# Attention and a two-layer MLP on one core: the SBUF pools allocated in another order

## The chip, the cores and the metric

One NeuronCore of one Trainium2 chip runs the kernel. The metric is the device time of one execution in microseconds (us); lower is better. Times of several runs are given by their median.

## What is computed

The reference takes `q`, `k`, `v` of shape (4, 8, 768, 64), two whole numbers `n_global` = 8 and `n_local` = 96, and two weight matrices. It computes masked attention, then an MLP over the 3072 x 512 result. Cut to what matters:

```
scores = q @ k.T / sqrt(64) + bias(head, distance)     # 1e9 below where not local or global
x      = softmax(scores) @ v                           # as 3072 x 512
h      = x @ w_in                                      # 512 x 2048, the first layer
g      = h * sigmoid(h)
out    = g @ w_out                                     # 2048 x 512, the second layer
```

The program calls this MLP the MoE part, hence the names.

## The kernel before, in words

**Tiles.** The 3072 tokens are 24 blocks `i` of 128, and two blocks make one of 12 groups `g` of 256 tokens. The weights are taken from HBM as 64-bit numbers and turned into a high part and a low part, each a float32r tile kept in SBUF for the whole run: `WIH` and `WIL` (lines 211, 212) for the first layer, `WOH`, `WOL` and two short tiles `w_last` for the second (line 219, `w_o`). The activations are split likewise, so every product is a sum of three matmuls: high with high, low with high, high with low.

**A matmul.** `nc.tensor.matmul(out, a, b)` first loads `a`, here always 128 columns, into the array as the stationary operand (the trace calls it LDWEIGHTS, on the row PEld) and then streams `b`, the moving operand, past it (MATMUL, on the row PE). The trace writes `out<-moving,stationary`.

**First layer.** `pair_h` (line 931, the matmuls are on line 938) has the weights `WIH` and `WIL` stationary and the 256 tokens of the group moving, from the tiles `xh` and `xl` made by `x_part` (line 696). For a pair of feature blocks there are 24 matmuls of 256 columns. The first two groups go through `moe_h` (line 831, matmuls on line 836), with the same operands.

**Gate.** `pair_tanh`, `pair_gate` and `pair_sum` (lines 942 to 956) make the gated activations in a tile `sg` on ScalarE (ACT), VectorE (DVE) and GpSimd (POOL); `pair_high` (line 965) and `pair_low` (line 971) split them into `gh` and `gl`.

**Second layer.** `pair_o` (line 986, matmuls on line 996) has `gh` or `gl` stationary and the weights moving: `WOH`, `WOL`, `w_last`, and sums of weights that are loaded from DRAM for each pair into `tx` and `ty`. Each is 256 columns wide, apart from 72 of 512 columns. The first two groups go through `moe_o` (line 856, matmuls on line 861, 512 columns) with `ghs` and `gls` stationary.

**Attention.** `stack_scores` (line 573, matmuls on line 580) streams `KH` and `KL`, 232 columns (128 in the first block of a batch), past `QH`, `QL` and `R`; each pair of heads lies 928 bytes after the one before in `KH` and `KL`. `turn` and `turn_p` transpose with the tile `ident` moving; `values` multiplies with `v`.

**Order.** A planner (`Plan`, line 50) with a cost and a rank for each step fixes, while the program is built, the order in which every engine gets its instructions. Nothing in it depends on where a tile lies. All large DMAs are issued on the SP queue.

**Places.** Each `tile_pool` takes a stretch of SBUF in every partition, and the stretches lie one behind the other in the order in which the pools are made (lines 196 to 204: `flag`, `const`, `sb2`, `sb3`). In a pool, the tiles of each tag lie behind those of the tag that was asked for first, and a size is rounded up to 32 bytes. A place below is a number of bytes in a partition, modulo 512.

Of the kernel before, what the change touches and what calls it, by code (L numbers as in the profile page):

```python
# [10 lines left out]
F32 = mybir.dt.float32  # L11
F32R = mybir.dt.float32r
BF16 = mybir.dt.bfloat16
I16 = mybir.dt.int16
I32 = mybir.dt.int32
# [6 lines left out]
P = 128  # L22
NPREV = 96
NG = 8
WIN = NPREV + NG + P
# [155 lines left out]
def attn_moe(ctx, tc, q, k, v, n_global, n_local, w_in, w_out, out):  # L181
    nc = tc.nc
    B, H, S, D = q.shape
    NT, DM = out.shape
    DFF = w_in.shape[1]
    NHP = H // 2
    NJ = S // P
    NCC = DM // P
    NFC = DFF // P
    NB = 2  # L190
    GT = NB * P
# [8 lines left out]
    ctx.enter_context(fast)  # L200
    ctx, outer = fast, ctx
    const = ctx.enter_context(tc.tile_pool(name="const", bufs=1))
    sb2 = ctx.enter_context(tc.tile_pool(name="sb2", bufs=2))
    sb3 = ctx.enter_context(tc.tile_pool(name="sb3", bufs=3))
    psum = ctx.enter_context(tc.tile_pool(name="psum", bufs=1, space=PSUM))
    dram = ctx.enter_context(tc.tile_pool(name="dram", bufs=1, space=bass.MemoryType.DRAM))

# [11 lines left out]
    def w_o(i, f):  # L219
# [5 lines left out]
                const.tile([P, NLAST, DM], F32R, name=f"w_last{x}", tag=f"last{x}") for x in range(2)  # L225
            )
        return last_w[i][:, f - (NFC - NLAST)]
    NM = const.tile([P, B * NJ * H], F32, name="NM")
    banks = [psum.tile([P, 512], F32, name=f"bank{i}") for i in range(8)]

    def bank(b, n=None, c=None):
# [3 lines left out]
        return x[:, :n] if c is None else x[:, :n * c].rearrange("p (n c) -> p n c", n=n)  # L235


    B1 = const.tile([P, NHP, WIN], BF16, name="B1")
    B0 = const.tile([P, NHP, P], BF16, name="B0")

    st = {}
    raw = const.tile([P, 2, 2], I32, name="raw")
    nc.gpsimd.memset(raw, 0)

    def scalars():
# [6 lines left out]

    def places():

        t1 = sb2.tile([P, 1024], F32, name="t1", tag="xh")
        t2 = sb2.tile([P, 1024], F32, name="t2", tag="xl")
        bias_t.extend(t1[:, i * WIN:(i + 1) * WIN] for i in range(3))
        bias_t.extend(t2[:, i * P:(i + 1) * P] for i in range(3))
        st["ones"] = [t2[:, i * P:(i + 1) * P] for i in (3, 4)]
        R, col = bias_t[0], bias_t[3]  # L260
        io = dict(allow_small_or_imprecise_dtypes=True)
        nc.gpsimd.iota(R[:, cur], [[-1, P]], base=0, channel_multiplier=1, **io)
        nc.gpsimd.iota(col, [[1, P]], base=0, channel_multiplier=0, **io)
        nc.gpsimd.iota(R[:, prev], [[-1, NPREV]], base=NPREV, channel_multiplier=1, **io)
        for x, c in zip(st["ones"], (1.0, 4294967296.0)):
            nc.gpsimd.memset(x, c)
# [47 lines left out]


    assert H == 8
    few = const.tile([P, 32], F32, name="few")
    assert B * NJ - PAR["VC"] // 2 <= 20
    VT, twice = few[:, :B * NJ - PAR["VC"] // 2], few[:, 20:21]
    nc.vector.memset(twice[:D], 1.0)  # L320
# [2 lines left out]
    def bias_of(first, hp):  # L323
        eng = nc.gpsimd if hp >= PAR["BP"][first] else nc.vector
        o, x = ((B0, bias_t[5]) if first else (B1, bias_t[2]))
        eng.tensor_scalar(o[:, hp], x, -(2.0 ** (-8.0 * (2 * hp + 1) / H)) / SC, None, ALU.mult)

    TOP = const.tile([P, 2, 2 * NFC], I16, name="TOP")  # L330
    first_gh = sb2.tile([P, NB, GT], F32R, name="ghs", tag="GH", bufs=1)
    first_gl = sb2.tile([P, NB, GT], F32R, name="gls", tag="GL", bufs=1)
    first_th = [sb2.tile([P, 2, 2 * GT], F32, name=f"ths{x}", tag="SG") for x in range(2)]
    lent_pt = [first_th[0][:, 1], first_th[1][:, 0], first_th[1][:, 1]]
    warm = first_th[0][:, 0, :P].bitcast(BF16)
    nc.vector.memset(warm, 0.0)
# [3 lines left out]
        SG=2, GH=1, GL=1, str=2, ty=2, ob=2, tt=3, ck=1,  # L340
# [47 lines left out]
    def lent(n):  # L388
        return n % 5 - 3 if n < PAR["NX"] and n % 5 > 2 else None
# [42 lines left out]
    for n in range(2 * NFC):  # L432
        rank = PAR["C0"] + PAR["CR"] * n
        a, m, x = [] if lent(n) is not None else [Buf("big")], Buf("mid", "m"), lent(n)
# [15 lines left out]
    def check(n, i):  # L450
        top = st["c", n].bitcast(I16).rearrange("p f w -> p (f w)").rearrange("p (f w) -> p f w", w=4)[:, :, 3]
        nc.vector.tensor_reduce(
            TOP[:, i, n:n + 1], top, AX.X, (ALU.min, ALU.max)[i], apply_absolute_value=True
        )
# [31 lines left out]
    xt = {}  # L486
# [112 lines left out]
    def cols(i):  # L599
        return (0 if i % NJ else C1), (WIN if i % NJ else P)  # L600
# [13 lines left out]
    def top_of(i, hp, a):  # L614
        t = blk[i]
        if not a:
            x = sb3.tile([P, 512], F32, name="pe", tag="m", bufs=NM2)
            t["p", hp] = x[:, :2 * WIN].rearrange("p (a n) -> p a n", a=2)
            x = sb3.tile([P, 4], F32, name="sm", bufs=4)
            t["sum", hp], t["inv", hp] = x[:, :2], x[:, 2:]  # L620
        h, n = 2 * hp + a, cols(i)[1]
        nm = NM[:, i * H + h:i * H + h + 1]
        nc.vector.tensor_tensor_reduce(  # L623
            t["p", hp][:, a, :n], t["s", hp][a][:, :n], B1[:, hp] if i % NJ else B0[:, hp],
            -SC / (1 + a), 3.0e38, ALU.add, ALU.min, nm,
        )

    def expo(i, hp, a):
        t = blk[i]
        h, x = 2 * hp + a, t["p", hp][:, a, :cols(i)[1]]  # L630
        nc.scalar.activation(  # L631
            x, x, AF.Exp, bias=NM[:, i * H + h:i * H + h + 1], scale=-1.0,
            accum_out=t["sum", hp][:, a:a + 1],
# [62 lines left out]
    def x_part(i, x):  # L696
        g, jj = divmod(i, NB)
        if (x, g) not in xt:
            xt[x, g] = sb2.tile([P, NHP, GT], F32R, name=x)
        return xt[x, g][:, :, jj * P:(jj + 1) * P]  # L700

    def x_high(i):
# [15 lines left out]
    for i in range(B * NJ):  # L718
        j, g = i % NJ, i // NB
        rank = NHP * i - PAR["QB"]  # L720
        ob, kk, lr = o_k[i], kb[i], PAR["LB"]
        if not i:
            xn, later = dict(k=Buf("qkn", "m"), q=Buf("qkn", "m")), []
            for p0, p1 in PARTS:
                for nm in "kq":
                    n, tp = p1 - p0, Buf("tq")
# [50 lines left out]
        for hp in range(NHP):  # L777
# [4 lines left out]
            n = cols(i)[1]  # L782
# [16 lines left out]
            for a in range(2):  # L799
                x = op("DVE", 318 if j else 210, u, (lambda i=i, hp=hp, a=a: top_of(i, hp, a)),  # L800
                       [o, o_b[j == 0, hp], before.get("top") if not a else None], [s[a % len(s)], pe])
# [18 lines left out]
        if early:  # L820
            x = Buf("pt", "m")
# [7 lines left out]
    mo = {}  # L829
# [110 lines left out]
                )  # L940

    def pair_tanh(g, n):
        mo["sg", g, n] = x = sb2.tile([P, 8, P], F32, name="sg", tag="SG")
        nc.scalar.activation(  # L944
            x[:, 0:4].rearrange("p (a b) c -> p a (b c)", a=2), mo["ph", g, n], AF.Tanh, scale=0.5
        )
# [11 lines left out]
    def off(g, n):  # L958
        return int(g >= SW[n])

    def pair_high(g, n, a=0, b=7):
        if not a:
            mo["gh", g, n] = sb2.tile([P, 7, P], F32R, name="gh", tag="GH", bufs=1)
        o = off(g, n)
        nc.scalar.copy(mo["gh", g, n][:, a:b], mo["sg", g, n][:, a + o:b + o])  # L965

    def pair_low(g, n, a=0, b=7):
        if not a:
            mo["gl", g, n] = sb2.tile([P, 7, P], F32R, name="gl", tag="GL", bufs=1)
        o = off(g, n)  # L970
        nc.vector.tensor_sub(  # L971
            mo["gl", g, n][:, a:b], mo["sg", g, n][:, a + o:b + o], mo["gh", g, n][:, a:b].bitcast(F32)
        )
# [73 lines left out]
    for g in range(NGRP):  # L1047
# [3 lines left out]
        for f in range(NFC) if g < G0 else ():  # L1051
            rank = 1e3 + (max(g, 1) * NFC + f + (PAR["LAG"] + 0.5 if g else 0))
            ph, th, gh, gl = Buf("h"), Buf("th"), Buf("gh"), Buf("gl")
# [17 lines left out]
        for n in range(NFC // 2) if g >= G0 else ():  # L1071
            rank = 1e3 + (g * NFC + 2 * n + PAR["LAG"] + 0.5)
            ph, sg, gh, gl, xs = Buf("h"), Buf("SG"), Buf("GH"), Buf("GL"), Buf("str", "big")
# [14 lines left out]
            for m, (a, b) in enumerate(cuts):  # L1088
                if b == 7:
                    for e in range(4):  # L1090
                        x = "DVE" if end else "POOL"
# [9 lines left out]
            if not std:  # L1101
                gg, nn = divmod(g * NFC // 2 + n - 2, NFC // 2)
                kept = [*o_t[n], *([o_h[gg, 2 * nn]] if gg >= G0 else [])]
                xl = op("DMA", 1456, r, (lambda g=g, n=n: x_load(g, n)), [*kept, before.get("x")], [xs], PAR["DL"])
# [77 lines left out]
    for u, o in o_s.items():  # L1182
        g, m = divmod(u, NB * NHP)
        f = (g - 1) * NFC + m * NFC // (NB * NHP) - PAR["AHEAD"]
# [5 lines left out]

    def judge():
        ok = few[:, 21:26]
        wx = sb2.tile([P, B * NJ * H], F32, name="wx", tag="SG")
        ng, nl = par[:, 0:1], par[:, 1:2]
        v = nc.vector
        v.tensor_scalar(ok[:, 0:1], ng, float(NG), None, ALU.is_le)
        yield
        v.tensor_scalar(wx, NM, 5.0e8, None, ALU.is_le)
        yield
        v.tensor_scalar(TOP[:, 0], TOP[:, 0], 16.0 * 984 + 1, None, ALU.is_ge)  # L1200
        yield
        v.scalar_tensor_tensor(ok[:, 0:1], nl, 1.0, ok[:, 0:1], ALU.is_ge, ALU.mult)
        yield
        v.scalar_tensor_tensor(wx, NM, -1.0e30, wx, ALU.is_ge, ALU.mult)
        yield
        v.scalar_tensor_tensor(TOP[:, 0], TOP[:, 1], 16.0 * 1064, TOP[:, 0], ALU.is_lt, ALU.mult)
        yield
        v.scalar_tensor_tensor(ok[:, 0:1], nl, NPREV + 1.0, ok[:, 0:1], ALU.is_le, ALU.mult)
        yield
        v.tensor_reduce(ok[:, 1:2], wx, AX.X, ALU.min)  # L1210
        yield
        v.tensor_reduce(ok[:, 2:3], TOP[:, 0], AX.X, ALU.min)
        yield
        v.memset(ok[:, 3:4], 1.0)
        yield
        v.tensor_scalar(VT, VT, 65536.0, None, ALU.is_le)
        yield
        v.tensor_reduce(ok[:, 4:5], VT, AX.X, ALU.min)
        yield
        v.tensor_mul(ok[:, 1:2], ok[:, 1:2], ok[:, 4:5])  # L1220
        yield
        v.tensor_mul(ok[:, 0:1], ok[:, 0:1], ok[:, 1:2])
        yield
        v.tensor_mul(ok[:, 0:1], ok[:, 0:1], ok[:, 2:3])
        yield
        v.tensor_scalar(ok[:, 0:1], ok[:, 0:1], 0.0, None, ALU.is_equal)
        st["ok"] = ok
        yield
# [9 lines left out]
    for n, o in enumerate(o_cd):  # L1238
        g, f = divmod(3 * NFC + PAR["CF"] + PAR["CN"] * n, NFC)
# [182 lines left out]
```

## Time and profile before

| | |
|---|---|
| median of 3 runs | 700.61 us (700.59 to 700.84) |
| the profiled execution | 700.56 us |
| its span, first to last instruction | 698.6 us |
| around the span | 1.96 us |
| granted TensorE clock, mean over the span | 0.996 |

The profile is of one execution. "Busy" is the time in which an engine had an instruction under way. Matmuls overlap and their ends are modelled, so a busy PE says little of its pace: the distance from the start of one matmul to the start of the next does, and it is called a step below. [...]

### The profile page before, as it was taken

The numbers are of one execution on the slowest core, as the hardware profiler recorded it, in microseconds if no ns is written. First come the engines' busy times: TensorE is split into PE (matmuls) and PEld (weight loads), VectorE is DVE, ScalarE is ACT, GpSimd is POOL, SyncE is SP. The second block draws the span as 40 slices with busy tenths as digits, with TensorE's granted clock in tenths as the row PEclk, the third lists the DMA queues.
The fourth block names the chain that finished last, engine by engine and source line by source line (L and its number), as shares of the span: only waits on it lengthen the run. The fifth ranks groups of instructions, "written<-read, shape, count | busy, mean of one in ns | idle before, by whom it ended". The sixth has DMA issues, their size and how long they took to land. (4 is left out here: it accounts for less than half of the span.)

```text
span 698.6 us, 15610 instructions
## 1 busy us (share of the span) xinstructions
PE 683.5 (98%) x5774; PEld 652.9 (93%) x5774; DVE 541.9 (78%) x1449; ACT 421.8 (60%) x941; POOL 153.5 (22%) x351
## 2 busy tenths in 40 slices
PE   8999999999999999999999999999999999999995
PEld 6778899899999999999999999999999999999994
DVE  6999999988688887877868878877777877664533
ACT  6976445686665576665665665765567656662321
POOL 2100000000122323223323232223323223323330
PEclk9999999999999999999999999999999999999998
DMA  9986657477699868748668667577757778542621
GB/s 186 242 260 233 206 180 244 154 249 236 198 292 305 251 208 229 235 151 257 198 190 245 189 184 250 165 231 219 212 172 223 223 187 229 172 156 101 209 95 35
DMA packets 146648, 143.25 MB, mean 205 GB/s; under 512 B 88420, under 2 KB 115556, under 8 KB 146564
## 3 DMA queue, kind: packets, MB, share of 16 engines
q1 hardware_dynamic: 146560, 142.17, 68.2%
q8 instruction: 47, 0.77, 0.4%
q14 instruction: 37, 0.30, 0.1%
q10 hardware_dynamic: 4, 0.00, 0.0%
HBM read 119.01 MB, written 18.87 MB: 197 GB/s over the span
## 5 line engine op out<-in xcount | busy, mean ns | idle before, releaser
L956 POOL TENSOR_TENSOR sg<-sg 128x128 f32<-128x128 f32 x292 | 130.8, 469 | 320.8 <-DVE sg L950 288.0
L938 PE MATMUL bank<-xh,WIH 128*128 128x256 f32 x640 | 186.2, 291 | 0.0
L938 PE MATMUL bank<-xh,WIL 128*128 128x256 f32 x640 | 180.3, 282 | 0.0
L938 PE MATMUL bank<-xl,WIH 128*128 128x256 f32 x640 | 180.0, 281 | 0.0
L971 DVE TENSOR_TENSOR gl<-sg,gh 128x896 fp32r<-128x896 f32 (+1 forms) x81 | 85.0, 1050 | 55.2 <-ACT gh L965 54.8
L938 PEld LDWEIGHTS bank<-xh,WIH 128*128 128x128 f32 x640 | 120.8, 189 | 0.7 <-issue 0.3
L938 PEld LDWEIGHTS bank<-xl,WIH 128*128 128x128 f32 x640 | 121.2, 189 | 0.3
L938 PEld LDWEIGHTS bank<-xh,WIL 128*128 128x128 f32 x640 | 120.1, 188 | 0.0
L631 ACT ACTIVATE pe<-pe,NM 128x232 f32<-128x232 f32 (+1 forms) x192 | 90.3, 473 | 38.3 <-DVE NM L623 35.3
L965 ACT CAST gh<-sg 128x896 fp32r<-128x896 f32 (+1 forms) x81 | 73.4, 907 | 48.5 <-POOL sg L956 37.2
L623 DVE CUSTOM_DVE_ANT_0 pe<-bank,B 128x232 f32<-128x232 f32 (+1 forms) x192 | 67.3, 373 | 35.3 <-PE bank L580 32.7
L944 ACT ACTIVATE sg<-bank 128x512 f32<-128x512 f32 x80 | 47.9, 598 | 44.2 <-PE bank L938 41.4
L996 PE MATMUL bank<-WOH,gh 128*128 128x256 f32 (+1 forms) x280 | 73.9, 293 | 0.0
L996 PE MATMUL bank<-WOL,gh 128*128 128x256 f32 (+1 forms) x280 | 73.0, 290 | 0.0
L950 DVE SCALAR_TENSOR_TENSOR sg<-sg,bank 128x512 f32<-128x512 f32 x80 | 54.8, 685 | 11.0 <-ACT sg L944 10.0
L647 DVE TENSOR_SCALAR pe<-pe,sm 128x232 f32<-128x232 f32 (+1 forms) x192 | 62.0, 361 | 1.5
L671 ACT COPY pt<-bank 128x512 f32<-128x512 f32 (+1 forms) x82 | 44.9, 550 | 29.2 <-PE bank L661 28.6
L661 PE MATMUL bank<-ident,pe 128*128 128x128 f32 (+1 forms) x352 | 55.1, 276 | 2.6 <-DVE pe L647 2.3
L996 PEld LDWEIGHTS bank<-WOH,gh 128*128 128x128 f32 x280 | 52.8, 189 | 0.9 <-issue 0.2
L996 PEld LDWEIGHTS bank<-WOL,gh 128*128 128x128 f32 x280 | 52.8, 189 | 0.7
L996 PE MATMUL bank<-tx,gh 128*128 128x256 f32 x296 | 49.2, 285 | 0.8 <-DMA tx<-ts 0.8
L996 PE MATMUL bank<-WOH,gl 128*128 128x256 f32 (+1 forms) x280 | 49.9, 294 | 0.0
(161 smaller groups left out, 1509.8 us busy)
## 6 DMA issues: line engine op xcount, KB each, us to landing
tx<-ts SPq DMA_DIRECT2D x74, 512.0 KB
ty<-ts SPq DMA_DIRECT2D x74, 256.0 KB
c<-in_moe_w_in_dram SPq DMA_DIRECT2D x16, 512.0 KB
c<-in_moe_w_out_dram SPq DMA_DIRECT2D x16, 512.0 KB
vn<-in_v_dram SPq DMA_DIRECT2D x24, 256.0 KB
w<-in_moe_w_in_dram SPq DMA_DIRECT2D x12, 512.0 KB
w<-in_moe_w_out_dram SPq DMA_DIRECT2D x12, 512.0 KB
kn<-in_k_dram SPq DMA_DIRECT2D x23, 256.0 KB
```

What stands on the lines that cost most here:

```text
L623: nc.vector.tensor_tensor_reduce(t["p", hp][:, a, :n], t["s", hp][a][:, :n], B1[:, hp] if i % NJ else B0[:, hp], -SC / (1 + a), 3.0e38, AL ...
L631: nc.scalar.activation(x, x, AF.Exp, bias=NM[:, i * H + h:i * H + h + 1], scale=-1.0, accum_out=t["sum", hp][:, a:a + 1],)
L647: nc.vector.tensor_scalar(x, x, t["inv", hp][:, a:a + 1], None, ALU.mult)
L661: nc.tensor.transpose(ps[:n, c, a], pe[:, a, c0:c0 + n], ident)
L671: nc.scalar.copy(t["pt", hp][:, c], t["tp", hp][:, c])
L938: nc.tensor.matmul(ph[:, a], w[:, cc, fs], x[:, cc], start=not cc and not m, stop=cc == NCC - 1 and m == 2)
L944: nc.scalar.activation(x[:, 0:4].rearrange("p (a b) c -> p a (b c)", a=2), mo["ph", g, n], AF.Tanh, scale=0.5)
L950: nc.vector.scalar_tensor_tensor(x, x, 1.0, mo["ph", g, n], ALU.add, ALU.mult)
L956: (eng.tensor_sub if e else eng.tensor_add)(x[:, o], x[:, a], x[:, b])
L965: nc.scalar.copy(mo["gh", g, n][:, a:b], mo["sg", g, n][:, a + o:b + o])
L971: nc.vector.tensor_sub(mo["gl", g, n][:, a:b], mo["sg", g, n][:, a + o:b + o], mo["gh", g, n][:, a:b].bitcast(F32))
L996: nc.tensor.matmul(o, l, r, start=(g, b) not in opened, stop=n == NFC // 2 - 1 and m == 2 and (p in (6, 5, 3, 4) or p == (b, 1)), skip_gro ...
```

## The change

The two pools `const` and `sb2` are cut up and the pieces put between and behind `sb3`. The new order is `const`, `sb3`, `con1`, `gate`, `con2`, `sbx`, `con3`, `sb2`, `small`. `raw` is made four times as large and only its first quarter is used. No instruction is added, taken away or moved, and every tile has the shape, the number of buffers and the users that it had.

```
     const = ctx.enter_context(tc.tile_pool(name="const", bufs=1))
+    sb3 = ctx.enter_context(tc.tile_pool(name="sb3", bufs=3))
+    con1 = ctx.enter_context(tc.tile_pool(name="con1", bufs=1))
+    gate = ctx.enter_context(tc.tile_pool(name="gate", bufs=2))
+    con2 = ctx.enter_context(tc.tile_pool(name="con2", bufs=1))
+    sbx = ctx.enter_context(tc.tile_pool(name="sbx", bufs=2))
+    con3 = ctx.enter_context(tc.tile_pool(name="con3", bufs=1))
     sb2 = ctx.enter_context(tc.tile_pool(name="sb2", bufs=2))
-    sb3 = ctx.enter_context(tc.tile_pool(name="sb3", bufs=3))
+    small = ctx.enter_context(tc.tile_pool(name="small", bufs=4))
...
-    NM = const.tile([P, B * NJ * H], F32, name="NM")
+    NM = con2.tile([P, B * NJ * H], F32, name="NM")
...
-    B1 = const.tile([P, NHP, WIN], BF16, name="B1")
-    B0 = const.tile([P, NHP, P], BF16, name="B0")
+    B1 = con3.tile([P, NHP, WIN], BF16, name="B1")
+    B0 = con3.tile([P, NHP, P], BF16, name="B0")
...
-    raw = const.tile([P, 2, 2], I32, name="raw")
+    raw = con1.tile([P, 8, 2], I32, name="raw")[:, :2]
...
-    few = const.tile([P, 32], F32, name="few")
+    few = con2.tile([P, 32], F32, name="few")
...
-    TOP = const.tile([P, 2, 2 * NFC], I16, name="TOP")
+    TOP = con3.tile([P, 2, 2 * NFC], I16, name="TOP")
...
-            x = sb3.tile([P, 4], F32, name="sm", bufs=4)
+            x = small.tile([P, 4], F32, name="sm")
...
-            xt[x, g] = sb2.tile([P, NHP, GT], F32R, name=x)
+            xt[x, g] = sbx.tile([P, NHP, GT], F32R, name=x)
...
-        mo["sg", g, n] = x = sb2.tile([P, 8, P], F32, name="sg", tag="SG")
+        mo["sg", g, n] = x = gate.tile([P, 8, P], F32, name="sg", tag="SG")
...
-            mo["gh", g, n] = sb2.tile([P, 7, P], F32R, name="gh", tag="GH", bufs=1)
+            mo["gh", g, n] = gate.tile([P, 7, P], F32R, name="gh", tag="GH", bufs=1)
...
-            mo["gl", g, n] = sb2.tile([P, 7, P], F32R, name="gl", tag="GL", bufs=1)
+            mo["gl", g, n] = gate.tile([P, 7, P], F32R, name="gl", tag="GL", bufs=1)
```

The lines left out do the same to `ghs`, `gls`, `ths`, `t1`, `t2` and `wx`, which share the places of `gh`, `gl`, `sg`, `xh`, `xl` and `sg`.

The places, added up from the sizes in the code, as bytes past that of `WIH`, modulo 512:

| tiles | before | after |
|---|---|---|
| `WIH`, `WIL`, `WOH`, `WOL` | 0 | 0 |
| `w_last` | 352 | 0 |
| `gh`, `gl`, `sg` (and `ghs`, `gls`) | 352 | 64 |
| `xh`, `xl` | 352 | 448 |
| tiles of `sb3` (`tx`, `ty`, `R`, `pe`, `pt`, `kn`, `qn`) | 96 | 0 |
| `KH`, `KL` (first pair of heads) | 352, 480 | 384, 0 |
| `QH`, `QL` | 96 | 128 |

A slice of a tile that a matmul of the two layers takes lies a multiple of 512 bytes behind its start, so the table holds for all of them. With the place of the stationary operand subtracted from that of the moving one, the difference is, before: 352 in the first layer; 160 for `WOH` and `WOL`, 256 for `tx` and `ty`, 0 for `w_last` in the second. After, it is 448, that is -64, for all of them.

## Rows read from the trace of the kernel before

**Rows 1.** The page: span, busy time of each engine (share, instructions).

```profile
span 698.6 us, 15610 instructions
PE 683.5 (98%) x5774; PEld 652.9 (93%) x5774; DVE 541.9 (78%) x1449; ACT 421.8 (60%) x941; POOL 153.5 (22%) x351
```

**Rows 2.** Busy time by stage (columns: us, then each engine), granted clock, DMA share.

```profile
25.00:150.00 125.00, 121.68 (x894) 106.42 (x891) 123.69 (x344) 79.49 (x206) 3.58 (x6) 1.00 0.70 217
150.00:650.00 500.00, 499.17 (x4395) 489.56 (x4393) 381.17 (x967) 311.37 (x659) 134.02 (x300) 1.00 0.70 211
650.00:698.60 48.60, 40.04 (x334) 39.57 (x332) 18.91 (x33) 12.19 (x17) 10.98 (x25) 0.95 0.37 121
```

**Rows 3.** Waits of PE over the whole span (us in total, times, longest).

```profile
PE bank L661 <- DVE pe L647: 2.3, 4, 0.8
...
PE bank L996 <- DMA tx<-ts: 0.8, 1, 0.8
```

**Rows 4.** Timeline of PE, first layer (start us, us, engine, line, operands).

```profile
303.26 0.28 PE L938 MATMUL bank<-xl,WIH 128*128 128x256 f32 x1
...
305.17 0.29 PE L938 MATMUL bank<-xh,WIL 128*128 128x256 f32 x1
```

**Rows 5.** Timeline of weight loads in the same stretch.

```profile
303.26 0.19 PEld L938 LDWEIGHTS bank<-xh,WIL 128*128 128x128 f32 x1
303.38 0.19 PEld L938 LDWEIGHTS bank<-xh,WIH 128*128 128x128 f32 x1
303.50 0.19 PEld L938 LDWEIGHTS bank<-xl,WIH 128*128 128x128 f32 x1
```

**Rows 6.** Timeline of PE: scores with 128 columns, then second layer.

```profile
305.36 0.27 PE L580 MATMUL bank<-KH,R 128*128 128x128 f32 x1
...
305.69 0.34 PE L996 MATMUL bank<-WOH,gh 128*128 128x256 f32 x1
305.87 0.28 PE L996 MATMUL bank<-WOL,gh 128*128 128x256 f32 x1
...
306.58 0.28 PE L996 MATMUL bank<-WOL,gh 128*128 128x256 f32 x1
```

**Rows 7.** Timeline of PE, second layer where tx and w_last alternate.

```profile
373.18 0.40 PE L996 MATMUL bank<-tx,gh 128*128 128x256 f32 x2
...
374.86 0.28 PE L996 MATMUL bank<-w_last,gl 128*128 128x256 f32 x1
```

**Rows 8.** Busy time and count of L938, then of L996, from 150 us on.

```profile
150.00:698.60 548.60, 258.03 (x1896) 237.71 (x1896) 1.00 0.67 203
...
150.00:698.60 548.60, 225.04 (x1626) 204.38 (x1626) 1.00 0.67 203
```

**Rows 9.** Timeline of PE: last score matmul and the next start, four places.

```profile
169.76 0.27 PE L580 MATMUL bank<-KL,R 128*128 128x232 f32 x1
169.87 0.40 PE L996 MATMUL bank<-WOH,gh 128*128 128x512 f32 x1
...
615.47 0.27 PE L580 MATMUL bank<-KL,R 128*128 128x232 f32 x1
615.58 0.29 PE L996 MATMUL bank<-WOH,gh 128*128 128x256 f32 x1
...
176.75 0.28 PE L580 MATMUL bank<-KL,R 128*128 128x232 f32 x1
176.86 0.40 PE L996 MATMUL bank<-WOH,gh 128*128 128x512 f32 x1
...
622.59 0.28 PE L580 MATMUL bank<-KL,R 128*128 128x232 f32 x1
622.70 0.28 PE L996 MATMUL bank<-WOH,gh 128*128 128x256 f32 x1
```

**Rows 10.** Longest waits of DVE and ACT on each other, 150 to 650 us.

```profile
DVE gl L971 <- ACT gh L965: 36.6, 38, 2.9
ACT gh L965 <- POOL sg L956: 19.6, 22, 2.7
```

More of the change, by code (lines that the diff above doesn't have):

```diff
@@ L253, in places @@
     def places():
-        t1 = sb2.tile([P, 1024], F32, name="t1", tag="xh")
-        t2 = sb2.tile([P, 1024], F32, name="t2", tag="xl")
+        t1 = sbx.tile([P, 1024], F32, name="t1", tag="xh")
+        t2 = sbx.tile([P, 1024], F32, name="t2", tag="xl")
         bias_t.extend(t1[:, i * WIN:(i + 1) * WIN] for i in range(3))
@@ L326, in bias_of @@
         eng.tensor_scalar(o[:, hp], x, -(2.0 ** (-8.0 * (2 * hp + 1) / H)) / SC, None, ALU.mult)
-    TOP = const.tile([P, 2, 2 * NFC], I16, name="TOP")
-    first_gh = sb2.tile([P, NB, GT], F32R, name="ghs", tag="GH", bufs=1)
-    first_gl = sb2.tile([P, NB, GT], F32R, name="gls", tag="GL", bufs=1)
-    first_th = [sb2.tile([P, 2, 2 * GT], F32, name=f"ths{x}", tag="SG") for x in range(2)]
+    TOP = con3.tile([P, 2, 2 * NFC], I16, name="TOP")
+    first_gh = gate.tile([P, NB, GT], F32R, name="ghs", tag="GH", bufs=1)
+    first_gl = gate.tile([P, NB, GT], F32R, name="gls", tag="GL", bufs=1)
+    first_th = [gate.tile([P, 2, 2 * GT], F32, name=f"ths{x}", tag="SG") for x in range(2)]
     lent_pt = [first_th[0][:, 1], first_th[1][:, 0], first_th[1][:, 1]]
@@ L1192, in judge @@
         ok = few[:, 21:26]
-        wx = sb2.tile([P, B * NJ * H], F32, name="wx", tag="SG")
+        wx = gate.tile([P, B * NJ * H], F32, name="wx", tag="SG")
         ng, nl = par[:, 0:1], par[:, 1:2]
```

## The prediction

> **What bounds the kernel now.** I read the page first: PE is busy 98% of the span, the next engine, DVE, 78% [rows 1]. Busy PE is modelled, so the waits come next: over the whole span PE waited 2.3 us for its longest releaser and 0.8 us for a DMA [rows 3]. The stages show where another engine could be the bound. From 25 to 150 us, while the weights are split, DVE is busy 123.69 of 125 us, and PE cannot gain there what DVE does not give. [...]
>
> So the step, from one start to the next, is what to read. In the first layer 16 steps lie between 303.26 and 305.17 us, 119.4 ns each [rows 4]. [...] The weight load of the next matmul starts within the same 10 ns as the current one (303.26, 303.38 in both lists) [rows 4, 5]: the two operands are read from SBUF side by side, and this is the only thing that the change can touch. [...] Where `tx` and `w_last` alternate, 14 steps take 1.68 us, 120.0 ns each [rows 7].
>
> **The change, term by term.** It removes and adds no instruction and moves none on any queue; the planner's order does not depend on places. What it alters is the relation: the place of the moving operand less that of the weights loaded meanwhile, modulo 512. It was 352 in the first layer and 160, 256 or 0 in the second, and becomes 448 everywhere.
>
> *Does the relation matter at all?* In the second layer the step was 118.3 at 160 and 120.0 at 256 and 0 mixed [rows 6, 7], in the first 119.4 at 352 [rows 4]: up to 1.7 ns between them. None of these is 448. The trace has 448 in one place. The last score matmul of a pair of heads streams 232 columns from `KL` while `gh` is loaded for the second layer; by the 928 bytes between pairs the relation is 448 for the third pair and 352 for the fourth. There are twelve such steps at 448, the first and last at 169.76 and 615.47 us, and thirteen at 352, the first and last at 176.75 and 622.59 us [rows 9]. Single rows are rounded to 10 ns; over all, the starts give 111 ns at 448 and 115 ns at 352. The difference is 4 ns, good to some 2 ns, and 111 is already next to the floor of 110 [rows 6], so more may be hidden behind it.
>
> *First layer from 150 us:* 1896 matmuls [rows 8]. Bounds: nothing if the 4 ns do not carry over to 256 columns; 119.4 - 110 = 9.4 ns, 17.8 us, if every step falls to the floor. I take 4 ns, as the very relations that are exchanged here (352 for 448) showed it: 7.6 us.
>
> *Second layer from 150 us:* 1626 matmuls [rows 8], 72 of them of 512 columns, which I leave at nothing; 1554 remain. Its relations 160, 256 and 0 were not compared with 448 by any row. Bounds: nothing, and 119 - 110 = 9 ns, 14.0 us. I take half of the first layer's, 2 ns, as `WOH` and `WOL` (half of these matmuls) step 1 ns faster already: 3.1 us.
>
> *First two groups, to 150 us:* nothing. DVE covers it, with 123.69 of 125 us busy [rows 2]. Without that cover, 4 ns for the 384 matmuls of line 836 would be 1.5 us.
>
> *The rest, together:* the score matmuls, transposes and value matmuls get other relations too. With 128 columns they sit at the floor of 110 [rows 6], and 232 columns ranged from 111 to 115 [rows 9]; 240 score matmuls by at most 4 ns are 1 us either way, and I take nothing. The tiles that DMAs fill all move, to places 0 or 64 bytes past `WIH` where they were at 96 or 352; PE waited 0.8 us for such a transfer in all [rows 3], so a gain is at most that, and a loss is covered as long as the DMA share stays near 0.70 [rows 2]. Nothing.
>
> *Sum:* 7.6 + 3.1 = 10.7 us off the profiled execution's own 700.56 us, which is 0.05 below the median of the runs. That gives **690 us**. Its own range is 684 (6 and 3 ns instead of 4 and 2, 16 us) to 697 (2 and 0 ns, 3.8 us). Because PE waits for almost nothing in this stage, what a step loses the end loses; what would be late next is the gate, below.
>
> [...]
>
> **The rivals.**
>
> *No effect.* [...] For it: the relations 0, 256 and 352 are all within 0.6 ns of 120 [rows 4, 7]. Against: 160 is below them, and 448 below 352 on average. Time: 700.6 us. Chance 0.18. [...]
>
> *Down to the floor.* At 448 the two reads never meet, and each step ends as soon as the next weights are in. For it: the steps at 448 already stand 1 ns from the floor [rows 6, 9]. Time, all steps at 110 ns: 700.6 - 17.8 - 14.0 = 669 us; where half of the rest stays, 684. Chance 0.20.
>
> *Slower.* In a step 256 columns are streamed while 128 are loaded, so the moving address runs twice as fast. If it starts 64 bytes behind the load it overtakes it near the start of every matmul, when PE has nothing in hand yet, whereas at 352 it starts 160 bytes behind and meets it later. If a meeting at the start costs as much more as the forecast has it cost less (4 and 2 ns), the time is 700.6 + 10.7 = 711 us; it decides as soon as the first layer's mean step passes 119.4 ns. Against: 448 gave the shorter step at 232 columns [rows 9]. Range 702 to 711. Chance 0.14.
>
> *Given back.* The steps shorten, but the second layer then waits for `gh` and `gl`: in the main stage DVE already waits 36.6 us for ACT's `gh`, and ACT 19.6 us for POOL's sums [rows 10], a chain that the plan has timed for the present pace of PE. It decides if PE's waits, now a few us in all, grow by about 8. Against: ACT and DVE are busy 62% and 76% there [rows 2]. Time about 698 us. Chance 0.06.
>
> That the change does not do what it says is no rival worth a chance: the places follow from sizes in the code.
>
> **How the numbers follow.** About 0.2%, 1.4 us, is what a measurement of this kernel can tell from no change. The forecast has 0.42. Faster are the forecast, the floor and the part given back: 0.42 + 0.20 + 0.06 = 0.68. Within 0.2% is the case without effect, 0.18 less a little for small drifts: 0.18. Slower is 0.14. The range runs from 675 us, which leaves out the lower part of the floor case (0.08), to 704 us, which leaves out most of the slower one (0.10). As faster cases hold most of the chance, the likeliest one's own range is 684 to 697 us.
>
> **What would show it.** In the changed kernel's timeline, 16 undisturbed steps of line 938 should take about 1.85 us instead of 1.91 (115.4 ns), those of line 996 about 117 ns; the 128-column steps should stay at 110; the counts stay as they are; PE's waits stay within a few us; DVE stays at its 123 to 124 us from 25 to 150 us. [...] A step near 110 means the floor. Shorter steps with new waits of line 996 for `gh` or `gl` mean that the gate gave it back. The prediction is wrong in its main step if the first layer does not gain 2 ns or more per matmul.

## The result, and the profile after

The changed kernel takes 693.24 us (median of four runs) where the kernel before takes 700.73 us in the runs beside it: ratio 0.9877, 95% interval 0.9841 to 0.9914. One of the four runs took 739.09 us at a granted clock of 0.85 of full speed, and the ratio, like all ratios below, leaves such a run out and is that of the means (692.85 and 701.45 us), not of the medians. The forecast was 690. The profiled execution took 692.62 us, 7.94 less than that of before.

The page of the changed kernel, as [rows 1]: 8.1 us of span are gone, with the same instructions, and PE is as full as before.

```profile
span 690.5 us, 15610 instructions
PE 674.4 (98%) x5774; PEld 642.6 (93%) x5774; DVE 541.2 (78%) x1449; ACT 420.4 (61%) x941; POOL 153.4 (22%) x351
```

Its stages, as [rows 2] (columns: us, then PE, PEld, DVE, ACT, POOL with counts, granted clock, DMA share, GB/s).

```profile
25.00:150.00 125.00, 121.31 (x897) 105.07 (x894) 123.85 (x346) 79.41 (x206) 3.58 (x6) 1.00 0.71 218
150.00:650.00 500.00, 498.40 (x4454) 488.64 (x4453) 383.94 (x972) 312.50 (x662) 136.22 (x304) 1.00 0.71 214
650.00:690.50 40.50, 32.08 (x273) 31.61 (x272) 15.32 (x25) 9.73 (x14) 8.78 (x20) 0.95 0.33 113
```

The stage up to 150 us has not moved: three matmuls more (897 for 894), DVE still full. From 150 to 650 us PE starts 4454 matmuls where it started 4395, at the same granted clock of 1.00. The whole gain is pace.

Its two matmul lines from 150 us on, first layer (now line 944), then second (now 1002), as [rows 8].

```profile
150.00:690.50 540.50, 251.88 (x1896) 232.13 (x1896) 1.00 0.68 206
...
150.00:690.50 540.50, 222.37 (x1626) 202.16 (x1626) 1.00 0.68 206
```

The first layer needs 258.03 - 251.88 = 6.15 us less, the second 225.04 - 222.37 = 2.67 us less: 8.8 us, of which 8.1 reach the end. The difference is in the next list, PE's waits over the whole span (us in total, times, longest), as [rows 3].

```profile
PE bank L667 <- DVE pe L653: 2.3, 4, 0.8
...
PE bank L1002 <- DMA tx<-ts: 1.3, 1, 1.3
...
PE bank L518 <- DVE sg L956: 0.3, 1, 0.3
```

The transfer into `tx` is waited for 1.3 us instead of 0.8, and a wait of a transpose for its bank, which the gate frees on DVE, is new: by the starts that step takes 0.55 us. PE's longest releaser stands at the same 2.3 us. Behind PE the chain of the gate has tightened from 150 to 650 us, as [rows 10] (36.6 and 19.6 us before), without reaching PE:

```profile
DVE gl L977 <- ACT gh L971: 37.7, 39, 3.0
...
ACT gh L971 <- POOL sg L962: 23.6, 23, 2.8
```

Now the steps themselves. The timeline of PE in the changed kernel shows the run of [rows 4] first, then the stretch of [rows 6], then another run of the first layer a group later (columns: start us, us, engine, line, operands).

```profile
301.96 0.28 PE L944 MATMUL bank<-xl,WIH 128*128 128x256 f32 x1
...
303.78 0.28 PE L944 MATMUL bank<-xh,WIL 128*128 128x256 f32 x1
...
304.06 0.28 PE L586 MATMUL bank<-KL,QL 128*128 128x128 f32 x1
304.18 0.28 PE L586 MATMUL bank<-KL,R 128*128 128x128 f32 x1
...
304.46 0.28 PE L1002 MATMUL bank<-WOL,gh 128*128 128x256 f32 x1
...
305.17 0.28 PE L1002 MATMUL bank<-WOL,gh 128*128 128x256 f32 x1
...
409.11 0.28 PE L944 MATMUL bank<-xl,WIH 128*128 128x256 f32 x1
...
411.70 0.28 PE L944 MATMUL bank<-xh,WIL 128*128 128x256 f32 x1
```

From 301.96 to 303.78 us lie 16 steps: 113.8 ns each, where [rows 4] had 119.4. From 409.11 to 411.70 us lie 22 steps of the same line, with the same operands at the same places: 117.7 ns each. The second layer steps 118.3 ns here (six steps, 304.46 to 305.17), as before, and is at 113.3 ns in other runs. So at one relation there are **two paces**. By the starts, most steps read 113, 113, 114 (113.3 on average) or 117 to 119 (117.8), and a run keeps the one it has settled into. Of the first layer's runs of nine or more matmuls, 51 of 96 leave at 113.3 (their last steps), of the second layer's 40 of 83. Over all undisturbed steps the mean is 116.1 ns in the first layer and 116.7 in the second. Neither pace is the forecast's 115.4: that is only near the mean of the two. In a second profile of the same kernel, 177 of 179 longer runs leave at the same pace as here: which one a run takes is not chance.

### The profile page after: what moved, and what is told of

It is laid out like the page before. It is cut to its first block, busy times and chain, and to the rows that moved or that the text cites. A ratio compares the mean times of both kernels' runs of the same rounds, so it can differ in the third digit from the quotient of the medians.

```text
span 690.5 us, 15610 instructions
## 1 busy us (share of the span) xinstructions
PE 674.4 (98%) x5774; PEld 642.6 (93%) x5774; DVE 541.2 (78%) x1449; ACT 420.4 (61%) x941; POOL 153.4 (22%) x351
## 5 line engine op out<-in xcount | busy, mean ns | idle before, releaser
L944 PE MATMUL bank<-xh,WIL 128*128 128x256 f32 x640 | 178.5, 279 | 0.0
L677 ACT COPY pt<-bank 128x512 f32<-128x512 f32 (+1 forms) x82 | 44.8, 549 | 27.3 <-PE bank L667 26.7
```

The lines of the kernel that those rows point to most:

```text
L677: nc.scalar.copy(t["pt", hp][:, c], t["tp", hp][:, c])
L944: nc.tensor.matmul(ph[:, a], w[:, cc, fs], x[:, cc], start=not cc and not m, stop=cc == NCC - 1 and m == 2)
```

## The experiments

Three theories were set against each other first. A: the relation, moving operand less weights, sets the step. B: it is enough that both operands lie at multiples of 64 bytes. C: places do not matter, and something else that moved (a tile that a DMA fills, the scores) made the gain. In the tables of steps the first ones of each run, before it settles, are left out.

**A bench of the relation.** Only matmuls, 16 relations with 6 runs of 36 each, weights fixed and moving operand shifted; the attention and the MLP are left out. Each relation has a `lambda` of its own in the list `mm`, and so a line of its own in the trace. In front of each run stands one short matmul, of 64 columns before the first run and 24 more before each next. `mo` and `so` count columns of 4 bytes.

```
+        lambda o, a, b, s, e: nc.tensor.matmul(o, a, b, start=s, stop=e),
...
+        for x, (mo, so, w) in enumerate(CASES):
+            for r in range(REPS):
+                m = 64 + 24 * r
+                nc.tensor.matmul(banks[7][:, :m], st[:, so:so + P], st[:, 8192 + mo:8192 + mo + m], start=True, stop=True)
+                for i in range(NMM):
...
+                    mm[x](
+                        banks[b][:, :w], st[:, so + f * P:so + f * P + P], st[:, 8192 + mo + c * 512:8192 + mo + c * 512 + w],
```

> This kernel leaves out attention and the MLP: it only runs matmuls of 128 x 256 columns in float32r, 216 for each of 16 relations (place of the moving operand less that of the weights, modulo 512: 0, 32, ... 480), in six runs of 36 behind a short matmul of another width. Theory A, the relation alone sets the step: the step differs between relations in a smooth curve, about 120 ns at 0 and 352, 118 to 119 at 160 and 256, and 113 to 118 at 448, which is at or near the lowest. Theory B, what counts is that both operands start at a multiple of 64 bytes (they do after the change, and xh, gh, tx did not before): the eight relations that are multiples of 64 all step alike, 113 to 118 ns, and the eight odd multiples of 32 all step about 120. Theory C, neither: all sixteen step alike within 0.5 ns.

The groups of this bench by line (line 24 + n has relation 32 n: 24 is 0, 26 is 64, 30 is 192, 32 is 256, 35 is 352, 38 is 448).

```profile
L35 PE MATMUL bank<-st 128*128 128x256 f32 x216 | 26.7, 283 | 0.0
L32 PE MATMUL bank<-st 128*128 128x256 f32 x216 | 26.7, 284 | 0.0
L24 PE MATMUL bank<-st 128*128 128x256 f32 x216 | 26.7, 284 | 0.0
...
L26 PE MATMUL bank<-st 128*128 128x256 f32 x216 | 26.1, 281 | 0.0
...
L30 PE MATMUL bank<-st 128*128 128x256 f32 x216 | 25.8, 280 | 0.0
L38 PE MATMUL bank<-st 128*128 128x256 f32 x216 | 25.8, 280 | 0.0
```

Here the mean of one (third figure from the right) hides the matter, since matmuls overlap; the busy time before it shows it: 26.7 - 25.8 = 0.9 us over 216 matmuls, 4.2 ns. Mean steps from the starts, in ns:

| relation | 0 | 32 | 64 | 96 | 128 | 160 | 192 | 224 |
|---|---|---|---|---|---|---|---|---|
| and + 256 | 256 | 288 | 320 | 352 | 384 | 416 | 448 | 480 |
| step | 119.9 | 117.3 | 117.1 | 120.0 | 119.0 | 117.8 | 115.6 | 118.3 |

Each column's two relations agree within 0.1 ns: the period is 256 bytes, not the 512 of the prediction. 448 is the shortest, and it is short as a mean of two paces: three of its six runs settle at 113.3, three at 117.8. It is the same three at 192 and at 448, and again at 192 in the later benches of this width: those behind the short matmuls of 64, 112 and 184 columns (the finer bench has no sixth run). So what went before a run picks its pace. 352 is the longest. B falls here: 0 and 128 are multiples of 64 and long.

**One layer at a time.** Same tiles, pools in other orders. In the first kernel only the first layer is at 448; the second has 192 for `WOH` and `WOL`, 256 for `tx` and `ty`, 0 for `w_last`. In the other only the second layer is at 448, the first stays at 352.

```
+    conb = ctx.enter_context(tc.tile_pool(name="conb", bufs=1))
+    conl = ctx.enter_context(tc.tile_pool(name="conl", bufs=1))
     gate = ctx.enter_context(tc.tile_pool(name="gate", bufs=2))
...
+    sb3 = ctx.enter_context(tc.tile_pool(name="sb3", bufs=3))
...
-                const.tile([P, NLAST, DM], F32R, name=f"w_last{x}", tag=f"last{x}") for x in range(2)
+                conl.tile([P, NLAST, DM], F32R, name=f"w_last{x}", tag=f"last{x}") for x in range(2)
```

> First layer at 448 as after the change; second layer at 192 (WOH, WOL), 256 (tx, ty), 0 (w_last), close to before. Every tile of the two layers starts at a multiple of 64 bytes. Theory A (relation): line of the first layer at a mean step of 116 ns, second layer as before at 118 to 120; of the 8 us gained the first layer's 1896 matmuls keep about 6 to 7, so 694 to 695 us, ratio about 0.991. Theory B (multiples of 64): both layers are short, 692 to 693 us, ratio 0.988.

```
-    NM = con2.tile([P, B * NJ * H], F32, name="NM")
+    NM = con2.tile([P, B * NJ * H + 8], F32, name="NM")[:, :B * NJ * H]
...
-    few = con2.tile([P, 32], F32, name="few")
+    few = con3.tile([P, 32], F32, name="few")
```

> Second layer at 448 as after the change; first layer back at 352 (its xh and xl at an odd multiple of 32). Theory A (relation): first layer back at 119 to 120 ns, second layer at 116 to 117; 1554 matmuls times 2 ns are 3 us, so 697 to 698 us, ratio about 0.996. Theory B gives the same here, as xh is off 64. Rival, the second layer alone brings the gain: 692 to 693 us.

Both lines from 150 us on in the kernel with only the first layer at 448.

```profile
150.00:691.30 541.30, 252.13 (x1896) 232.25 (x1896) 1.00 0.67 205
...
150.00:691.30 541.30, 224.11 (x1626) 203.44 (x1626) 1.00 0.67 205
```

The same in the kernel with only the second layer there.

```profile
150.00:693.90 543.90, 258.03 (x1896) 237.33 (x1896) 0.99 0.67 204
...
150.00:693.90 543.90, 220.28 (x1626) 200.27 (x1626) 0.99 0.67 204
```

The first takes 693.45 us, ratio 0.9907 (0.9892 to 0.9922): its first layer gains 258.03 - 252.13 = 5.90 us; the second gains 0.93, most of it in `WOH` and `WOL`, which are at 192 and step 1 ns less than before. The other takes 696.21 us, ratio 0.9942 (0.9929 to 0.9956): a first layer of 258.03 us to the hundredth, and a second that gains 4.76. Each layer answers to its own relation, so C falls. But the second layer gains 4.76 us alone and only 2.67 in the changed kernel, at the same relation. With the first layer at its 120 ns, 65 of the second's 83 longer runs leave at 113.3, in the changed kernel 40. So the second layer's pace depends on more than its own relation. The difference lies in the 31 of the 83 runs that start right behind a run of the first layer: here 29 of them leave at 113.3, in the changed kernel 1.

**The same relations, all places 32 bytes further.**

```
-    ident = const.tile([P, P], F32, name="ident")
+    ident = const.tile([P, P + 8], F32, name="ident")[:, :P]
```

> The changed kernel with every tile behind the identity moved on by 32 bytes: all relations stay 448, every operand of the two layers starts at an odd multiple of 32. Theory A (relation): as after the change, 692 to 694 us, ratio 0.988. Theory B (multiples of 64): as before, 700 to 701 us, ratio 1.000.

```profile
150.00:689.00 539.00, 251.97 (x1896) 232.19 (x1896) 1.00 0.68 206
...
150.00:689.00 539.00, 222.43 (x1626) 202.19 (x1626) 1.00 0.68 206
```

693.48 us, ratio 0.9907 (0.9892 to 0.9922), and both lines within 0.1 us of the changed kernel: B is out in the kernel too. The times of this kernel and of the one with only the first layer at 448 (693.45) cannot be told apart; their lines of the second layer can, 222.43 for 224.11 us.

**Finer, and other widths.** The same bench in steps of 8 bytes (4 near 64 and 192), then with 512 and 232 columns.

```
-REPS, NMM = 6, 36
+REPS, NMM = 5, 36
...
-REPS, NMM = 6, 36
+REPS, NMM = 4, 24
```

> Matmuls alone again (attention and the MLP are left out), 180 for each of 40 relations from 0 to 248 in steps of 8 bytes, and of 4 bytes around 64 and 192, in five runs of 36. The first sweep had the same step at r and r + 256, so 0 to 248 covers all. Theory A1: steps depend on the 32-byte block alone; then relations between two multiples of 32 step like one of the two, and nothing is under 113.3 ns. Theory A2: there is a narrow best place near 192 (448 modulo 256), with all five runs at 113.3 or even near the floor of 110, where the 32-byte grid only touches its edge (at 192 itself half of the runs stood at 113.3, half at 117.8). Rival: between the grid points the step is as mixed as at 192, so the mode a run falls into is set by what went before, not by the place.

> Matmuls alone again: 96 of 512 columns and then 96 of 232 columns for each of the relations 0 to 224 in steps of 32. [...]

None of the three readings set out for the finer bench held: no place near 192 is better than 192, and the best place, 112, was not foreseen. In steps of 8 bytes most relations lie at 116 to 121 ns, but 112 settles at 113.3 in every run after some 8 steps (mean 113.5), and 8 and 104 are at 125.3 and 126.0, means of runs at 120 and runs at 127 or 130. With 512 columns relation 0 is the *shortest*, 226.7 ns, 64 is at 230.0, 128 at 232.6 and all others at 233.3 to 234.3. With 232 columns nothing is left: 111.6 to 111.7 ns at seven relations, 112.4 at 192, where single steps run from 107 to 118 in a repeating pattern.

**112 and 8 in the kernel.** The four large weights in one tile, 16 bytes late, so that the first layer and `WOH`, `WOL` are at 112; then 24 bytes late, with the first layer at 8.

```
+    NI, NO = NCC * DFF, (NFC - NLAST) * DM
+    W = const.tile([P, 2 * (NI + NO) + 8], F32R, name="W")
+    WIH, WIL = (W[:, 4 + x * NI:4 + (x + 1) * NI].rearrange("p (c f) -> p c f", c=NCC) for x in range(2))
...
+    WIH, WIL = (W[:, 6 + x * NI:6 + (x + 1) * NI].rearrange("p (c f) -> p c f", c=NCC) for x in range(2))
```

> All weights in one tile that begins 16 bytes late, pools in a third order: the first layer and the WOH and WOL half of the second stand at 112 (modulo 256), the place where all five runs of the sweep stepped at 113.3 ns; tx, ty and w_last at 192. Theory A (the relation modulo 256 sets which steps are possible): first layer at 113.4 to 114.5 ns instead of 116.1 after the change, WOH and WOL at 114 to 115, so 1737 x 6 + 768 x 4 + 740 x 2 ns = 15 us less PE time than before, 1 to 2 us of it given back in waits: 685 to 687 us, ratio 0.978 to 0.981, faster than the changed kernel by 6 to 8 us. Rival, the entry into a run decides (runs in the kernel are only 3 to 24 matmuls long, in the sweep 36): first layer still near 116, 691 to 694 us.

> The same with the weights 24 bytes late: the first layer stands at 8 (modulo 256), where four of five runs of the sweep stepped at 126.7 ns; WOH and WOL at 120 (sweep: 120 to 121 ns), tx, ty and w_last at 192. Theory A: first layer at 125 to 127, second at 117 to 120; 1737 x 6 ns = 10 to 12 us more than before, so 709 to 713 us, ratio 1.013 to 1.018. Rival, the gain of the change came from the order of the pools in another way (transfers landing elsewhere, DVE or ACT): 691 to 701 us.

The first layer's line with the weights 16 bytes late, then 24 bytes late, one line of each kernel.

```profile
150.00:696.20 546.20, 257.09 (x1896) 236.74 (x1896) 1.00 0.68 203
```

```profile
150.00:699.30 549.30, 255.08 (x1896) 234.74 (x1896) 0.99 0.68 203
```

Both were misses: 699.23 us, ratio 0.9973 (0.9960 to 0.9986), and 699.42 us, 0.9977 (0.9967 to 0.9988). By the starts the first layer steps 119.0 ns at "112" and 117.8 at "8", not 113.5 and 125. In the second kernel the second layer, with `WOH` and `WOL` at 120, takes 227.73 us, 2.7 more than before, which uses up what the first gains. Its time lies in the range of the rival named with it, the order of the pools, but C had already fallen with the kernels of one layer each. The relation alone does not carry from the bench to the kernel. In the bench the moving operand had been off the grid of 32 bytes, here the weights were. The changed kernel, timed beside these two:

> The changed kernel itself, on the same chip as the two others, to set them against each other: 692 to 694 us, ratio 0.988 to 0.991, first layer near 116 ns and second near 116.7.

692.25 us, ratio 0.9883 (0.9866 to 0.9900).

**Relation and grid apart.** From the misses came theory D: where each operand stands to a grid of 32 bytes counts beside the relation. The bench with weights 16 bytes late at 16 relations, and with 112 and 192 at other shifts of both (the list is one line in the kernel).

```
+CASES = [(4, 4, 256), (8, 4, 256), (12, 4, 256),
...
+    (28, 0, 256), (48, 0, 256), (36, 8, 256), (56, 8, 256),
...
+    (30, 2, 256), (50, 2, 256), (8, 6, 256), (34, 6, 256)]
```

> Matmuls alone (attention and the MLP are left out), 216 for each of 28 pairs of places. In the kernel with the weights 16 bytes late the first layer stepped at 119 ns at the relation 112, where the sweep, whose weights began on a multiple of 32 bytes, had 113.3. First 16 cases: weights 16 bytes off the 32-byte grid, relations 0 to 240 in steps of 16. Theory D (where each operand stands to a 32-byte grid counts beside the relation): with the weights off the grid 112 steps at 118 to 120 and the whole curve differs from that of weights on the grid, by 2 ns or more at some relations. Theory A (the relation alone): 113.3 at 112, 113.3 or 117.8 at 192, as before, and it was the kernel's short runs that kept it at 119. Then the controls: relations 112 and 192 with the weights 0, 32, 64 and 128 bytes on: 113.3 at 112 and 113.3 or 117.8 at 192 by both theories; 8 bytes on, and 8 and 112 with the weights 24 bytes on: theory A 126.7 at 8, theory D something else (the kernel had 117.9).

The groups by line. Line 36 is relation 192 and line 31 relation 112, both with the weights 16 bytes late; lines 40 and 41 are 112 and 192 with the weights on the grid, line 42 is 112 with both a further 32 bytes on, line 49 is 192 with the weights 8 bytes late.

```profile
L49 PE MATMUL bank<-st 128*128 128x256 f32 x216 | 26.7, 284 | 0.0
...
L31 PE MATMUL bank<-st 128*128 128x256 f32 x216 | 26.6, 285 | 0.0
...
L41 PE MATMUL bank<-st 128*128 128x256 f32 x216 | 25.8, 280 | 0.0
...
L42 PE MATMUL bank<-st 128*128 128x256 f32 x216 | 25.5, 278 | 0.0
...
L40 PE MATMUL bank<-st 128*128 128x256 f32 x216 | 25.5, 278 | 0.0
L36 PE MATMUL bank<-st 128*128 128x256 f32 x216 | 25.4, 277 | 0.0
```

D holds. Relation 112 is at 113.4 ns with the weights on the grid and 119.7 with them 16 bytes late, the arrangement of the miss, which had 119.0. Relation 8 with the weights 24 bytes late is at 117.6; the other miss had 117.8. Relation 192 goes from 115.6 on the grid to 120.0 with both 8 bytes off, and to 113.3 with both 16 off. That last case is better than the change: all its six runs settle at 113.3, after five or six steps. At 112 and 192, shifts of both by 32, 64 or 128 bytes alter nothing: each group takes 25.5 us at 112 and 25.8 at 192.

**Two kernels from the bench.** `xh` and `xl` become slices of one tile, 16 bytes late, with the first layer at 112 and the weights on the grid; then `WIH` and `WIL` 16 bytes late too, at 192. The second layer keeps the grid of the change and, modulo 256, its relation in both.

```
-            xt[x, g] = sbx.tile([P, NHP, GT], F32R, name=x)
+            if not xt:
+                st["X"] = sbx.tile([P, 4 * NHP * GT + 8], F32R, name="x", tag="X", bufs=1)
+            y = 4 + (2 * (x == "xl") + (g + 1) % 2) * NHP * GT
+            xt[x, g] = st["X"][:, y:y + NHP * GT].rearrange("p (h t) -> p h t", h=NHP)
...
+    W = conw.tile([P, 2 * NCC * DFF + 8], F32R, name="W")
```

> The changed kernel with the tiles xh and xl 16 bytes late, in one tile, and the pools shifted so that the first layer has relation 112 with the moving operand 16 bytes off the 32-byte grid and the weights on it; the second layer stays at 192 on the grid. Theory D (relation and grid together decide; measured as the case of offsets 112 and 0, which settled at 113.3 ns after some 8 steps): a run of 24 first-layer matmuls has 8 steps of about 118 and 16 of 113.3, mean 114.9 ns, 1.1 below the changed kernel's 116.0, so 1737 x 1.1 = 1.9 us less: about 690.8 us, ratio to the kernel before 0.986. Rival (the short runs of the kernel between other matmuls do not settle as the long ones do): first layer at 117 to 119 ns as it was with the weights late, 695 to 699 us, ratio 0.992 to 0.998.

> The same, but with WIH and WIL 16 bytes late as well: relation 192 in the first layer with both operands 16 bytes off the 32-byte grid; the second layer stays at 192 on the grid. Theory D (the case of offsets 208 and 16 settled at 113.3 ns in each of its six runs after some 5 steps, where 192 and 0 did so in three of six): 5 steps of 118 and 19 of 113.3, mean 114.3 ns, 1.7 below the changed kernel's 116.0, 1737 x 1.7 = 3.0 us less: about 689.7 us, ratio 0.984. Theory A (the relation alone decides): 116.0 ns as in the changed kernel, 692.5 us, ratio 0.988. Rival (short runs do not settle): 116 to 118 ns, 692.5 to 696 us.

Both lines at 112.

```profile
150.00:690.90 540.90, 252.71 (x1896) 232.85 (x1896) 1.00 0.68 206
...
150.00:690.90 540.90, 222.03 (x1626) 201.64 (x1626) 1.00 0.68 206
```

Both lines at 192 with both operands 16 bytes late.

```profile
150.00:687.00 537.00, 250.25 (x1896) 230.46 (x1896) 1.00 0.69 207
...
150.00:687.00 537.00, 220.25 (x1626) 200.12 (x1626) 1.00 0.69 207
```

At 112 the time is 693.08 us, ratio 0.9889 (0.9871 to 0.9907), no better than the change and not the 690.8 expected: 66 of the 96 longer runs leave at 113.3, but each needs some ten steps to get there, and 68 of these 96 have no more than 18 matmuls. At 192 with both 16 bytes late it is **689.77 us, ratio 0.985 (0.983 to 0.987)**, the shortest here; the changed kernel was not timed beside it, but the one at 112 was. It is next to the 689.7 expected, in part by luck: the first layer gains 1.63 us on the change (251.88 to 250.25), not 3.0, and the second layer, which was to stay, 2.12. Now 89 of the first layer's 96 leave at 113.3. The run that took 117.7 ns a step in the changed kernel is this one here (timeline of PE, 24 matmuls in one row, then the next start):

```profile
407.84 2.91 PE L950 MATMUL bank<-x,W 128*128 128x256 f32 x24
410.58 0.29 PE L1008 MATMUL bank<-WOH,gh 128*128 128x256 f32 x1
```

24 steps in 2.74 us are 114.2 ns. The second layer, not touched, gains too: 220.25 us for 222.37; 64 of 83 leave at 113.3. Of the 31 that start right behind a first-layer run it is now 30, for 1 in the changed kernel. It is not the pace itself that is handed on: in the changed kernel 17 of the 31 stand behind a run that had settled at 113.3 and all 17 leave at the slower pace, while with the first layer at 352, which never gets there, 29 of 31 leave at 113.3. What is handed on stays open.

## Why the prediction was right, point by point

**What bounds the kernel** held: the time fell by what the steps lost, with PE at 98% before and after.

**First layer, 4 ns and 7.6 us.** 6.15 us of 1896 matmuls are 3.2 ns. That the relation counts was right; that its size was close was luck, as the row it came from does not bear it. The 4 ns between `KL`,`R` steps at 448 and at 352 [rows 9] were taken as the price of the relation. They are there (110.5 and 114.1 ns by the starts), but the step just before makes up for them: from `KL`,`QL` to `gh` are 224.3 and 224.0 ns. The two lines that [rows 9] leaves out:

```profile
615.35 0.28 PE L580 MATMUL bank<-KL,QL 128*128 128x232 f32 x1
...
622.48 0.27 PE L580 MATMUL bank<-KL,QL 128*128 128x232 f32 x1
```

And the difference stays where it is when the places change. `KL` and `gh` moved so that the two relations became 256 and 160, and the same steps take 110.0 and 114.1 ns in the changed kernel:

```profile
609.12 0.28 PE L586 MATMUL bank<-KL,QL 128*128 128x232 f32 x1
609.24 0.27 PE L586 MATMUL bank<-KL,R 128*128 128x232 f32 x1
609.35 0.29 PE L1002 MATMUL bank<-WOH,gh 128*128 128x256 f32 x1
...
616.10 0.27 PE L586 MATMUL bank<-KL,QL 128*128 128x232 f32 x1
616.20 0.28 PE L586 MATMUL bank<-KL,R 128*128 128x232 f32 x1
616.32 0.29 PE L1002 MATMUL bank<-WOH,gh 128*128 128x256 f32 x1
```

So these 4 ns do not speak against the rival *No effect*: they are no price of the places, but time that one step leaves to its neighbour. The bench agrees, with means of 111.6 to 112.4 ns at 232 columns at all eight relations. What bears the gain is the bench with 256 columns: 352 is of the longest class, 120.0, and 448 of the shortest, 115.6.

**Second layer, 2 ns and 3.1 us.** 2.67 us of the 1554 matmuls of 256 columns are 1.7 ns. The halving was argued from `WOH` and `WOL` stepping 1 ns faster already; the bench agrees, with 160 at 117.8 and 256 and 0 at 119.9, though over the whole kernel before the gap is 0.4 ns (118.4 to 118.8 by the starts) and not 1. What it left out is the link between the layers: alone the second layer gains 4.76 us. So this term, too, came near partly by luck.

**First two groups, nothing.** Right, and shown: 362 undisturbed first-layer steps there lost 1.2 us by the starts, and the stage still ended with DVE, 123.85 of 125 us busy.

**The rest, nothing.** Slightly off: 0.94 us went back into two waits from 150 us on, by the starts: 0.50 for the `tx` transfer and 0.44 for the transpose's bank (0.55 us for a step that took 0.11 before). *Given back* named `gh` and `gl` for such a wait, and some 8 us of it; PE waits no longer for `gh` than before.

**The other rivals.** *No effect* on the whole is out by the two kernels with one layer each. Its argument, that 0, 256 and 352 are all within 0.6 ns of 120, was a true reading: modulo 256 these are two places, 0 and 96, which both step 120, and the trace of before held no 256-column step of the short class. In the benches steps of 256 columns range from a settled 113.3 to a mean of 126.0 ns with nothing altered but the places. *Down to the floor* did not come: the lowest settled step of 256 columns anywhere is 113.3, 3 ns over the 110 of [rows 6], and half of the runs in the changed kernel do not get there. That 110 is a floor was the author's estimate from the steps of 128 columns [rows 6]; in the first 10 us of the trace of before, steps of 2 columns (line 290, three from 4.50 to 5.14 us) and of 128 (line 512, four from 7.52 to 8.37 us) take 213 ns alike by the starts. *Slower* did not come at 448, though places at which the step is longer than 120 exist (8 and 104 in the bench, 125.3 and 126.0). Its moving address, twice as fast as the other, was the author's estimate from 256 and 128 columns a step [rows 4, 5], not a measurement.

**What stays open.** Why 192 modulo 256 is short, why there are two paces at one place, and what in SBUF or in the array has a period of 256 bytes and a grid of 32. The runs show that the places and the previous matmuls decide, not how: the forecast's two reads that meet were not tested.

## What to carry to other kernels

Where PE is bound by a row of equal matmuls, each with its own weight load, take the step from the starts, and look whether it differs between places or between runs of the same line. If so, sweep the distance between moving operand and weights over 256 bytes, with both operands on the grid of 32 bytes and 16 off it, at the kernel's own width and length of run; how many steps a place needs to settle counts as much as the pace it settles at (at 112 some ten steps ate up the gain). Then move pools until the hot pairs stand so, which costs no instruction (15610 here before and after), and expect part of the gain back in waits (0.94 us here).

## What was not expected

- Two stable paces, 113.3 and 117.8 ns, for the same operands at the same places; a run picks one in its first steps and keeps it, and picks the same one again in a second execution (177 of 179 longer runs).
- A period of 256 bytes in the relation (r and r + 256 agree within 0.1 ns), and, as far as tried, of 32 in the place of the pair (25.5 us at 112 and 25.8 at 192, at each of four places).
- 8 bytes between good and bad: 104 gives 126.0 ns and 112 gives 113.5.
- A step that looks 4 ns cheaper may only pass the time on to its neighbour: sum over both (224.3 and 224.0 ns).
- The order turns round with width: at 512 columns relation 0 is the best (226.7 ns) and 192 one of the worst (233.3 to 234.3); at 232 columns the place hardly matters (111.6 to 112.4).
